# Weight gradients in pairs of accumulators over half tiles, more of them in each slot, and early places for the first loads of the attention backward

## The chip, the cores and the metric

The kernel runs on one core of a Trainium2 chip. The metric is the time of one execution on the device in microseconds (us): the median of three runs before the change is 865.62 us (864.01 to 870.82). A profile is one further execution, recorded by the hardware profiler; its span goes from the first to the last instruction. The engines are named as in the profile: PE is the matrix engine (PEld its weight loads), DVE the vector engine, ACT the scalar engine, POOL the general engine, SP the engine that only issues transfers (SPq is its queue). Transfers are issued by SP and by POOL, and move over 16 DMA engines that both share.

## The reference

A transformer layer with sliding-window attention and a feed-forward block is run forward, and all gradients of it are taken backward, on 2048 tokens of 512 features (bf16). Cut to what is computed:

```python
def A(x, wqkv, wo):                       # S=2048, D=512, 32 heads of 16
    q, k, v = split(x @ wqkv)
    idx = pos[:, None] - arange(8) * 2     # window of 8 keys, 2 apart
    attn = softmax(masked(einsum(q, k[idx]) * scale))
    return einsum(attn, v[idx]) @ wo

def B(x, w1, b1, w2, b2):                 # F = 1792
    return gelu(x @ w1 + b1) @ w2 + b2

def f(x, wqkv, wo, w1, b1, w2, b2):
    h = x + A(layernorm(x), wqkv, wo)
    return h + B(layernorm(h), w1, b1, w2, b2)

out, vjp = jax.vjp(f, x, wqkv, wo, w1, b1, w2, b2)
return (out, *vjp(grad_out))              # output and 7 gradients
```

## The kernel before

The tokens go in four chunks of 512 (`NC`, `CH`), each of four row tiles of 128. There are three stages.

The first stage runs the attention forward and leaves its intermediates in DRAM: the layer-normed inputs `ln1_d` and `ln2_d`, the attention output `o_d`, and the rows of q, k and v. The transposed `ln2` of each chunk stays in SBUF (`ln2T`, four tiles of the pool `lnT`).

The second stage is the feed-forward block, forward (`p2_h`) and backward (`p2_rest`). It stores the activations `g` and the gradient of their inputs `gh`, turned to token-major by a transposing DMA (`tok_store`, L508: SP reads into `tst`, POOL stores), in `gT_d` and `ghT_d`. At its end stand the gradient rows `gh_all`.

The third stage is the attention backward (from L612), and within it the weight gradients. In it the order on every engine is the order of the code (`tc.manual_schedule`), in the second stage a scheduler sets it. For each chunk `c`, DVE multiplies `got` (the gradient times `wo` transposed, made by `p3_go`) with the values `vw` (L888), PE sums the products into `ps_ga` (L894), DVE makes `pp`, PE takes off the row sum (L941), and DVE makes `glf` (L949), the gradient of the logits, and from it the coefficients `cf`. Then come band tiles: for v, q and k four each, in which DVE multiplies gathered rows `R` with `cf` (L793, two instructions a tile) and PE sums them (L801); `R` is 1.3 MB, gathered by an indirect DMA that POOL issues (L250). With a chunk's q, k and v done, `gln1` two passes later multiplies them with the transposed `wqkv` (L856) and runs the layer-norm backward on DVE. There are `NC + 2` passes, c = 0 to 5.

The weight gradients are plain matmuls over all 16 token tiles and nothing waits for them but the end. A generator, `wgrads` (L649), yields after each matmul; `filler` (L729) runs it until an allowance of time is spent, and `slot` (L752) grants that allowance: the time of the DVE work just issued, times `RATIO` (1.22), less the estimated time of the PE work that falls due in the slot. `MM` (0.22 us) is what a matmul of 512 columns is charged. In `wgrads`, `yield 24.0` or `yield 14.0` behind a load spends the allowance without a matmul, and `yield "q"` stops it until a flag of that name is set. What is left runs at the end (`filler(1000.0)`).

The order of the weight gradients is `out_6` (called gw2 below: L657, 14 groups of 16 matmuls), the bias `out_7` (16), `out_4` (gw1: L678, 28 groups of 16 with 256 columns), `out_3` (gwo: L691, 4 groups), `out_2` (gwq: L715, 12 groups). A group sums in one PSUM bank of two (`psF`), ACT copies it to one of two tiles `gwst` (L633), and POOL stores it (L634). One operand is a whole token-major tensor of 2 MB in a single buffer `r16` (`gout`, then `ln2`, `o`, `ln1`), the other comes in tiles of 1 MB in two buffers `gwm`. The `ln1` tensor is loaded in 32 transfers (L698), because its rows are permuted.

At the start of the third stage SP issues the transposed loads of `wo` and `wqkv` (L619, L621), then `vw` and `ln1r`.

Of the kernel before, what the change touches and what calls it, by code (L numbers as in the profile page):

```python
# [10 lines left out]
P = 128  # L11
BF16 = mybir.dt.bfloat16
# [24 lines left out]
def kernel(  # L37
# [277 lines left out]
    ln2T = [lnT.tile([P, DC, CH], BF16, name=f"ln2T{c}") for c in range(NC)]  # L315
# [181 lines left out]
    late.release()  # L497
    ff = LP("ff", "right")
# [6 lines left out]
    gh_all = [None] * NC  # L505
    ps2 = [dict() for _ in range(NC)]

    def tok_store(src, f0, f1, dst, c):  # L508
        n = f1 - f0
        st = ff.tile([P, 16, P], BF16, name="tst", tag="tst", bufs=3)  # L510
        SY.dma_start_transpose(out=st[:, 0:4 * n, :], in_=src[:, 0:n, :].rearrange("p a n -> p (a n)"))
        G.dma_start(out=dst[:, f0:f1, c, :], in_=st[:, 0:4 * n, :].rearrange("p (a t) f -> p a (t f)", a=n))  # L512

    def p2_h(c):
        d = ps2[c]
        d["g"], d["d"] = [], []
        for (f0, f1) in FB:
            n = f1 - f0
            xb = ff.tile([P, 4, 512], BF16, name="xb", tag="xb", bufs=2)
            x2 = ff.tile([P, 4, 512], BF16, name="x2", tag="x2", bufs=2)  # L520
# [28 lines left out]
    def p2_rest(c):  # L549
        d = ps2[c]  # L550
        gts, dts = d["g"], d["d"]
        goT = ff.tile([P, DC, CH], BF16, name="goT", tag="goT", bufs=1)
        SY.dma_start_transpose(out=goT[:], in_=gof[c * CH:(c + 1) * CH, :])
        gout = ff.tile([P, TPC, D], BF16, name="gout", tag="gout", bufs=1)
        load_rows(gout, gof, c)
        ln2 = ff.tile([P, TPC, D], BF16, name="ln2r", tag="ln2r", bufs=1)
# [55 lines left out]
    lnT.release()  # L612
# [5 lines left out]
    woT = p3.tile([P, DC, D], BF16, name="woT")  # L618
    SY.dma_start_transpose(out=woT[:], in_=A_wo)  # L619
    wqkvT = p3.tile([P, 12, D], BF16, name="wqkvT")  # L620
    SY.dma_start_transpose(out=wqkvT[:], in_=A_wqkv)  # L621
    glf = p3.tile([P, 2, SP], BF16, name="glf")
    V.memset(glf[:, :, S:SP], 0.0)
# [6 lines left out]

    def wg_out(ps, dst, width=D, sca=1.0):
# [15 lines left out]
    MM = 0.22  # L647

    def wgrads():  # L649
        r16 = load_tm("gout_r", gof)  # L650
        tiles = [load_t(gT_d, f) for f in range(2)]
        yield 24.0
        for f in range(FT):
            gtm = tiles[f // 2]
            ps = FY("ps_gw2")
            for t in range(NT):
                T.matmul(ps[:], lhsT=gtm[:, f % 2, t, :], rhs=r16[:, t, :], start=(t == 0), stop=(t == NT - 1))  # L657
                yield MM
            if f % 2 == 1:
                n = f // 2 + 2  # L660
                tiles.append(load_t(gT_d, n) if n < 7 else load_t(ghT_d, n - 7))
            wg_out(ps, out_6[f * P:(f + 1) * P, :], D, 0.5)
        ps = FY("ps_gb2")
        for t in range(NT):
            T.matmul(ps[0:1, :], lhsT=ones_col[:], rhs=r16[:, t, :], start=(t == 0), stop=(t == NT - 1))
            yield MM
        r16 = load_tm("ln2_r", ln2_d)
# [3 lines left out]
        yield 14.0  # L671
        tiles = tiles[7:]
        for q in range(7):
            ghm = tiles[q]
            for dc in range(DC):
                ps = FY("ps_gw1")
                for t in range(NT):
                    T.matmul(ps[:, 0:256].rearrange("p (a f) -> p a f", a=2), lhsT=r16[:, t, dc * P:(dc + 1) * P], rhs=ghm[:, :, t, :],  # L678
                             start=(t == 0), stop=(t == NT - 1))
                    yield MM / 2  # L680
                if dc == DC - 1:
                    if q + 2 < 7:
                        tiles.append(load_t(ghT_d, q + 2))
                    if q == 6:
                        r16 = load_tm("o_r", o_d)
                wg_out(ps, out_4[dc * P:(dc + 1) * P, q * 256:(q + 1) * 256], 256)
        yield 14.0
        for k in range(DC):
            ps = FY("ps_gwo")
            for t in range(NT):  # L690
                T.matmul(ps[:], lhsT=r16[:, t, k * P:(k + 1) * P], rhs=gh_all[t // TPC][:, t % TPC, :],  # L691
                         start=(t == 0), stop=(t == NT - 1))
                yield MM
            wg_out(ps, out_3[k * P:(k + 1) * P, :])
        r16 = gwp.tile([P, NT, D], BF16, name="ln1_r", tag="r16", bufs=1)
        for sc in range(NC * 2):
            for j, ap in enumerate(perm_rows(ln1_d, sc * 256, sc)):
                SY.dma_start(out=r16[32 * j:32 * j + 32, 2 * sc:2 * sc + 2, :], in_=ap)  # L698
        HN = NT // 2

        def half(sel, i):
            t_ = gwp.tile([P, HN, D], BF16, name="gqh", tag="gwm", bufs=2)
            SY.dma_start(out=t_[:], in_=g3_d[sel][:, i * HN:(i + 1) * HN, :])
            return t_
        yield "q"
        hv = [half(0, 0), half(0, 1)]
        yield 14.0
        for si, sel in enumerate((0, 2, 1)):
            for d2 in range(2):
                pss = [FY("ps_gwq") for _ in range(2)]  # L710
                for i in range(2):
                    for dd in range(2):
                        dc = 2 * d2 + dd
                        for t in range(HN):
                            T.matmul(pss[dd][:], lhsT=r16[:, i * HN + t, dc * P:(dc + 1) * P], rhs=hv[i][:, t, :],  # L715
                                     start=(i == 0 and t == 0), stop=(i == 1 and t == HN - 1))
                            yield MM
                        if i == 1:
                            wg_out(pss[dd], out_2[dc * P:(dc + 1) * P, sel * D:(sel + 1) * D])
            if si < 2:  # L720
                yield ("v", "k")[si]
                hv = [half((2, 1)[si], 0), half((2, 1)[si], 1)]
# [23 lines left out]
    RATIO = 1.22  # L746
# [28 lines left out]
    def load_R():  # L775
# [5 lines left out]
        R = p3.tile([P, 10, 512], BF16, name="R", tag="rows", bufs=3)  # L781
# [3 lines left out]
    def band_tile(kind, c, sc, m, cf, gs, sca, after):  # L785
# [4 lines left out]
        pr = p3.tile([P, 2, 4, 512], BF16, name="prb", tag="prod", bufs=3)  # L790
        for hf in range(2):
            o = (2 - 2 * hf if kind == "q" else 2 * hf) + 4 * m
            V.tensor_tensor(out=pr[:, hf].rearrange("p j (d h) -> p j d h", h=H),  # L793
# [3 lines left out]
        def pe():  # L797
            ps = Y("ps_band")
            for hf in range(2):
                for j in range(4):  # L800
                    T.matmul(ps[32 * j:32 * j + 32, :], lhsT=S32[:], rhs=pr[:, hf, j, :],  # L801
# [11 lines left out]
    st3 = [dict() for _ in range(NC + 2)]  # L813

    def p3_go(c, at=(1, 2, 3, 4)):
        ghT = p3.tile([P, DC, CH], BF16, name="ghT", tag="ghT", bufs=1)
        got = p3.tile([P, 4, CH], BF16, name="got", tag="got", bufs=1)
# [213 lines left out]
```

## Time and profile before

| what | value |
| --- | --- |
| median of the runs | 865.62 us (864.01 to 870.82) |
| the profiled execution's own time | 867.38 us |
| its span | 865.6 us |
| mean granted clock of PE | 0.896 of full speed |
| busy: PE, DVE, ACT, POOL | 661.8, 531.1, 339.7, 196.7 us |
| moved by DMA | 160.99 MB |
| second stage ends, third begins | about 432 us |
| last DVE work | about 719 us |

Rows of the timeline give the start and the length of a group of neighbouring instructions in us, the engine, the line of the code, the operation, output and inputs, how often, and in brackets how long the engine sat idle before it and what ended that. Rows of the waits give the engine and line that waited, what it waited for, and the total in us, the number of times and the longest. Rows of the windows give a stretch in us and its length, the busy time (and number of instructions) of PE, PEld, DVE, ACT and POOL, then the granted clock, the busy share of the 16 DMA engines, and GB/s. Line numbers are those of the kernel before.

### The profile page before, as it was taken

What the parts mean: (1) busy time and instruction counts of PE and PEld (TensorE: products, weight loads), DVE (VectorE), ACT (ScalarE), POOL (GpSimd) and SP (SyncE); (2) the same over time, 40 slices, a digit from 0 to 9 for tenths busy, and PEclk for the clock granted to TensorE, in tenths of its full rate; (3) what the DMA queues carried; (4) which work ended last, traced back from release to release, by engine and by line L of the source; (5) the groups of instructions that cost most, each with busy time, mean ns of one, the idle gap of its engine ahead of it and who ended that gap; (6) DMA issues with size and microseconds to landing.
All of it is one profiled execution on the core that took longest, in us unless ns stands there. A gap on an engine that the chain in (4) does not pass through costs nothing. (4 is left out here: it accounts for less than half of the span.)

```text
span 865.6 us, 10398 instructions
## 1 busy us (share of the span) xinstructions
PE 661.8 (76%) x3948; PEld 300.8 (35%) x3948; DVE 531.1 (61%) x774; ACT 339.7 (39%) x529; POOL 196.7 (23%) x253
## 2 busy tenths in 40 slices
PE   4888786667899898889935479888886798753486
PEld 2334332222333333333412134333322457631232
DVE  6889796478768777775615996977975951000000
ACT  2558675576446345342132144353323342100011
POOL 3204243301102102102100623243251323200011
PEclk9999998787999999999967569999986899977699
DMA  8547376785549558547996388678479544332442
GB/s 304 205 152 223 120 248 220 179 177 132 90 117 231 122 106 221 133 108 210 191 292 231 115 293 293 224 228 319 170 247 368 159 148 150 115 116 82 137 159 103
DMA packets 143120, 160.99 MB, mean 186 GB/s; under 512 B 95469, under 2 KB 125982, under 8 KB 136414
## 3 DMA queue, kind: packets, MB, share of 16 engines
q1 hardware_dynamic: 124846, 74.83, 33.3%
q0 software_dynamic: 18224, 85.49, 28.9%
q8 instruction: 31, 0.51, 0.2%
q14 instruction: 19, 0.16, 0.1%
HBM read 87.63 MB, written 48.03 MB: 157 GB/s over the span
## 5 line engine op out<-in xcount | busy, mean ns | idle before, releaser
L793 DVE TENSOR_TENSOR prb<-R,cf 128x2048 bf16<-128x2048 bf16 x96 | 110.5, 1218 | 16.9 <-DMA R<-q_d,rowi 13.9
L526 PE MATMUL ps_h<-ln2T,w 128*128 128x512 bf16 x224 | 65.2, 420 | 21.3 <-ACT x L529 18.7
L801 PE MATMUL ps_band<-prb,S 128*32 128x512 bf16 x384 | 41.1, 461 | 38.6 <-DVE prb L793 38.3
L715 PE MATMUL ps_gwq<-gqh,ln_r 128*128 128x512 bf16 x192 | 44.0, 390 | 30.4 <-DMA gqh<-gq_d 25.7
L634 POOL DMA_DIRECT2D out_dram<-gwst x58 | 31.5, 544 | 145.5 <-ACT gwst L633 136.0
L574 PE MATMUL ps_gg<-goT,w2T 128*128 128x512 bf16 x224 | 54.5, 378 | 11.0 <-DVE gb1p L577 8.6
L678 PE MATMUL ps_gw<-gwm,ln_r 128*128 128x256 bf16 x448 | 53.7, 279 | 7.8 <-ACT gwst L633 7.8
L657 PE MATMUL ps_gw<-gout_r,gwm 128*128 128x512 bf16 x224 | 58.3, 400 | 0.0
L561 PE MATMUL ps_f<-w,gt 128*128 128x512 bf16 x224 | 55.8, 393 | 1.6 <-DVE gt L538 1.6
L528 ACT ACTIVATE xb<-ps_h,b1c 128x512 bf16<-128x512 f32 x56 | 38.2, 686 | 45.9 <-PE ps_h L526 45.2
L351 PE MATMUL ps_qkv<-ln1T,wqkv 128*128 128x512 bf16 x192 | 48.6, 393 | 6.3 <-ACT kt L353 2.0
L211 ACT ACTIVATE gyr<-ps_gl,rstd 128x512 bf16<-128x512 f32 x32 | 22.0, 687 | 73.0 <-PE ps_gl L856 35.1
L678 PEld LDWEIGHTS <-ln_r 128*128 128x128 bf16 x448 | 43.9, 100 | 17.7 <-issue 11.8
L512 POOL DMA_DIRECT2D gT_d<-tst x16 | 12.6, 786 | 156.4 <-DMA tst<-gt 152.1
L888 DVE TENSOR_TENSOR pr<-got,vw 128x4096 bf16<-128x4096 bf16 x16 | 35.9, 2286 | 17.2 <-DMA vw<-vf_d 17.2
L856 PE MATMUL ps_gl<-wqkvT,gqkvT 128*128 128x512 bf16 x192 | 44.1, 385 | 0.0
L526 PEld LDWEIGHTS <-w 128*128 128x128 bf16 x224 | 23.3, 105 | 56.7 <-issue 39.5
L633 ACT ACTIVATE gwst<-ps_gw 128x256 bf16<-128x256 f32 (+1 forms) x42 | 18.9, 456 | 57.6 <-DMA out_dram<-gwst 30.1
L288 DVE TENSOR_TENSOR prb<-R,cf 128x2048 bf16<-128x2048 bf16 x32 | 37.3, 1210 | 5.7 <-DMA R<-v_d,rowi 2.9
L803 ACT ACTIVATE gks<-ps_band 128x512 bf16<-128x512 f32 x32 | 19.0, 600 | 53.9 <-PE ps_band L801 48.0
L258 DVE TENSOR_TENSOR pr<-qt,kt 128x4096 bf16<-128x4096 bf16 x16 | 36.0, 2282 | 5.5 <-ACT qt L353 3.4
L529 ACT ACTIVATE x<-ps_h,b1c 128x512 bf16<-128x512 f32 x56 | 38.1, 685 | 1.4 <-DVE dt__2685 L543 0.4
(327 smaller groups left out, 1207.2 us busy)
## 6 DMA issues: line engine op xcount, KB each, us to landing
gwm<-gT_d SPq DMA_DIRECT2D x7, 1024.0 KB
gwm<-ghT_d SPq DMA_DIRECT2D x7, 1024.0 KB
gT_d<-tst POOLq DMA_DIRECT2D x12, 512.0 KB
ghT_d<-tst POOLq DMA_DIRECT2D x12, 512.0 KB
ln_d<-ln POOLq DMA_DIRECT2D x8, 512.0 KB
out_dram<-gwst POOLq DMA_DIRECT2D x30, 128.0 KB
w<-in_B_w_dram POOLq DMA_DIRECT2D x2, 1792.0 KB
vw<-vf_d SPq DMA_DIRECT2D x4, 528.0 KB
```

The costliest lines, as they stand in the source:

```text
L351: T.matmul(ps[:, gg, :], lhsT=wqkv[:, dc, sel * D + g * P:sel * D + (g + 1) * P], rhs=st_[c]["ln1T"][:, dc, :], start=(dc == 0), stop=(dc ...
L526: T.matmul(ps[:, i, :], lhsT=w1[:, dc, f * P:(f + 1) * P], rhs=ln2T[c][:, dc, :], start=(dc == 0), stop=(dc == DC - 1))
L528: A.activation(out=xb[:, f - f0, :], in_=ps[:, i, :], func=ACT.Identity, bias=b1c[:, f:f + 1])
L529: A.activation(out=x2[:, f - f0, :], in_=ps[:, i, :], func=ACT.Square, bias=b1c[:, f:f + 1])
L561: T.matmul(ps[:], lhsT=gts[f // 4][:, f % 4, j * P:(j + 1) * P], rhs=w2[:, f, :], start=(f == 0), stop=False)
L574: T.matmul(ps[:, i, :], lhsT=w2T[:, dc, f * P:(f + 1) * P], rhs=goT[:, dc, :], start=(dc == 0), stop=(dc == DC - 1))
L657: T.matmul(ps[:], lhsT=gtm[:, f % 2, t, :], rhs=r16[:, t, :], start=(t == 0), stop=(t == NT - 1))
L678: T.matmul(ps[:, 0:256].rearrange("p (a f) -> p a f", a=2), lhsT=r16[:, t, dc * P:(dc + 1) * P], rhs=ghm[:, :, t, :], start=(t == 0), stop ...
L715: T.matmul(pss[dd][:], lhsT=r16[:, i * HN + t, dc * P:(dc + 1) * P], rhs=hv[i][:, t, :], start=(i == 0 and t == 0), stop=(i == 1 and t == ...
L793: V.tensor_tensor(out=pr[:, hf].rearrange("p j (d h) -> p j d h", h=H), in0=R[:, o:o + 4, :].rearrange("p j (d h) -> p j d h", h=H), in1=c ...
L801: T.matmul(ps[32 * j:32 * j + 32, :], lhsT=S32[:], rhs=pr[:, hf, j, :], start=(hf == 0), stop=(hf == 1), skip_group_check=True)
L856: T.matmul(ps[:], lhsT=gqkv[c][:, b, j * P:(j + 1) * P], rhs=wqkvT[:, b, :], start=(b == 0), stop=(b == 11))
```

## The change

**Pairs and halves.** The whole-tensor operand comes in two halves of eight token tiles (`load_half`, `load_perm`) in three buffers `r8`. `mm_pair` sums two groups at a time in the two PSUM banks: the first token half for both groups, then the second half for both. So the first half's buffer is free, and the next load can be issued, before the pair is done. Both groups are copied and stored when the pair is done.

**More matmuls per slot.** `RATIO` goes from 1.22 to 1.4, and of the yields that spend allowance only 10.0 before gwq and the two 6.0 stay; 24.0, 14.0 and 14.0 go.

**Early places.** The transposed `wo` and the three parts of the transposed `wqkv` take the places of the `ln2T` tiles in `lnT` once those are read, and are loaded during the second stage (`load_wT`). `glf` has a pool of its own. `vw`, the two halves of `gout` and the first two tiles of `gT_d` are the first loads of the third stage. `ln1r` is loaded a row tile at a time in three buffers instead of a chunk at a time in one. Temporaries of the second stage are merged (`xa`) and get fixed shapes.

```diff
+    def lnt(name):
+        return lnT.tile([P, DC, CH], BF16, name=name, tag="ln2T", bufs=NC)
...
+    def load_wT(name, src):
+        wT[name] = lnt(name)
+        SY.dma_start_transpose(out=wT[name][:], in_=src)
...
     for c in range(NC):
+        if c == 2:
+            load_wT("woT", A_wo)
+            load_wT("wqT", A_wqkv[:, 0:D])
+        if c == 3:
+            load_wT("wkT", A_wqkv[:, D:2 * D])
+            load_wT("wvT", A_wqkv[:, 2 * D:3 * D])
...
-    woT = p3.tile([P, DC, D], BF16, name="woT")
-    SY.dma_start_transpose(out=woT[:], in_=A_wo)
-    wqkvT = p3.tile([P, 12, D], BF16, name="wqkvT")
-    SY.dma_start_transpose(out=wqkvT[:], in_=A_wqkv)
...
-    def load_tm(name, src):
-        r = gwp.tile([P, NT, D], BF16, name=name, tag="r16", bufs=1)
-        SY.dma_start(out=r[:], in_=src.rearrange("(t p) d -> p t d", p=P))
+    def load_half(name, src, i):
+        r = gwp.tile([P, HN, D], BF16, name=name, tag="r8", bufs=3)
+        SY.dma_start(out=r[:], in_=src[i * HN * P:(i + 1) * HN * P, :].rearrange("(t p) d -> p t d", p=P))
...
+    def mm_pair(name, mm, cost):
+        pss = [FY(name) for _ in range(2)]
+        for i in range(2):
+            for o in range(2):
+                for t in range(HN):
+                    mm(pss[o], o, i, t, dict(start=(i == 0 and t == 0), stop=(i == 1 and t == HN - 1)))
+                    yield cost
+        return pss
...
+    load_vw(0)
+    gout_r = [load_half("gout_r", gof, 0)]
+    tiles = [load_t(gT_d, 0)]
+    gout_r.append(load_half("gout_r", gof, 1))
+    tiles.append(load_t(gT_d, 1))
 
     def wgrads():
-        r16 = load_tm("gout_r", gof)
-        tiles = [load_t(gT_d, f) for f in range(2)]
-        yield 24.0
...
+        ln2_r = [load_half("ln2_r", ln2_d, 0)]
+        for q in range(7):
+            g_ = tiles[q]
+            pss = yield from mm_pair("ps_gw2", lambda ps, o, i, t, k: T.matmul(ps[:], lhsT=g_[:, o, i * HN + t, :], rhs=gout_r[i][:, t, :], **k), MM)
+            n = q + 2
+            tiles.append(load_t(gT_d, n) if n < 7 else load_t(ghT_d, n - 7))
...
+        ln2_r.append(load_half("ln2_r", ln2_d, 1))
+        o_r = [load_half("o_r", o_d, 0)]
...
-        yield 14.0
...
+        o_r.append(load_half("o_r", o_d, 1))
+        ln1_r = [load_perm("ln1_r", ln1_d, 0)]
+        for k2 in range(2):
+            pss = yield from mm_pair("ps_gwo", lambda ps, o, i, t, k: T.matmul(
...
+        ln1_r.append(load_perm("ln1_r", ln1_d, 1))
         yield "q"
-        hv = [half(0, 0), half(0, 1)]
-        yield 14.0
+        hv = [load_g3(0, 0), load_g3(0, 1)]
+        yield 10.0
...
-    RATIO = 1.22
+    RATIO = 1.4
...
-    def load_ln1(c):
-        st3[c]["ln1"] = p3.tile([P, TPC, D], BF16, name="ln1r", tag="ln1r", bufs=1)
-        load_rows(st3[c]["ln1"], ln1_d, c)
+    def load_ln1(t):
+        x = pt3("ln1r")
+        SY.dma_start(out=x[:], in_=ln1_d[t * P:(t + 1) * P, :])
+        ln1q.append(x)
```

**What moves, place by place.** On SP, at the end of the second stage; `tst` are the last transposed stores, `go_d` the rows of the first chunk's `got`, `gwm` the 1 MB tiles. Before:

```order
75 L511 DMA_TRANSPOSE tst<-dt__3324 128x8x128
76 L619 DMA_TRANSPOSE woT<-in_A_wo_dram 128x4x512
77 L621 DMA_TRANSPOSE wqkvT<-in_A_wqkv_dram 128x12x512
78 L870 DMA vw<-vf_d 128x4x528
79 L178 DMA ln1r<-ln_d 128x4x512
80 L241 DMA go_d_144<-tmst 128x2x512 x2
81 L638 DMA gout_r<-in_grad_out_dram 128x16x512
```

And now:

```order
80 L531 DMA_TRANSPOSE tst<-dt__3317 128x8x128
81 L705 DMA vw<-vf_d 128x4x528
82 L671 DMA gout_r<-in_grad_out_dram 128x8x512
83 L683 DMA gwm<-gT_d 128x4096
84 L671 DMA gout_r<-in_grad_out_dram 128x8x512
85 L683 DMA gwm<-gT_d 128x4096
86 L892 DMA ln1r<-ln_d 128x512 x2
87 L241 DMA go_d_144<-tmst 128x2x512 x2
```

The two transposed loads no longer stand ahead of `vw`, and the first operands of the weight gradients stand ahead of the stores of `go_d`. On SP near the end; `ln_r` are the permuted halves of `ln1`, `gqh` the halves of gq, gv and gk for gwq, `sh` the shifted logits' gradient that the last k bands need. Before:

```order
112 L643 DMA gwm<-ghT_d 128x4096 x5
113 L638 DMA o_r<-o_d 128x16x512
114 L698 DMA ln_r<-ln_d 32x2x512 x32
115 L703 DMA gqh<-gq_d 128x4096 x2
116 L703 DMA gqh<-gv_d 128x4096 x2
117 L703 DMA gqh<-gk_d 128x4096 x2
```

And now:

```order
123 L884 DMA sh<-attn 32x2x512 x4
124 L671 DMA o_r<-o_d 128x8x512
125 L678 DMA ln_r<-ln_d 32x2x512 x16
126 L892 DMA ln1r<-ln_d 128x512 x4
127 L678 DMA ln_r<-ln_d 32x2x512 x16
128 L689 DMA gqh<-gq_d 128x4096 x2
129 L884 DMA sh<-glf 32x2x512 x4
```

The loads for gwo and gwq now stand among those of the passes c = 3 and c = 4, ahead of the last `sh`. On POOL, during the k bands of pass c = 2, where the rows for the v bands of chunk 2 are gathered ahead (`R<-go_d_146`, from the second gather before and the first now); `gk_d` and `gv_d` are stores of band results, `gx` those of the layer-norm backward, `gwst` those of the weight gradients. Before:

```order
113 L250 DMA R<-go_d_146,rowi 128x5120
114 L806 DMA gk_d<-gks 128x1024
115 L634 DMA out_dram<-gwst 128x512
116 L862 DMA out_dram<-gx 128x512
117 L634 DMA out_dram<-gwst 128x512
118 L862 DMA out_dram<-gx 128x512 x2
```

And now:

```order
113 L250 DMA R<-go_d_146,rowi 128x5120
114 L667 DMA out_dram<-gwst 128x256 x2
115 L850 DMA gk_d<-gks 128x1024
116 L667 DMA out_dram<-gwst 128x256 x2
117 L250 DMA R<-go_d_146,rowi 128x5120
118 L850 DMA gk_d<-gks 128x1024
```

The stores of gw1 (256 columns) now stand between the gathers, two at a time, where single stores of gw2 stood.

More of the change, by code (lines that the diff above doesn't have):

```diff
@@ L497 @@
     late.release()
+    glp = LP("glp", "right")
+    glf = glp.tile([P, 2, SP], BF16, name="glf")
+    V.memset(glf[:, :, S:SP], 0.0)
     ff = LP("ff", "right")
@@ L645, in load_t, with load_g3 @@
         return t_
-    MM = 0.22
-    def wgrads():
-        r16 = load_tm("gout_r", gof)
-        tiles = [load_t(gT_d, f) for f in range(2)]
-        yield 24.0
[L653 to L662, printed above, removed]
+    def load_g3(sel, i):
+        t_ = gwp.tile([P, HN, D], BF16, name="gqh", tag="gwm", bufs=2)
+        SY.dma_start(out=t_[:], in_=g3_d[sel][:, i * HN:(i + 1) * HN, :])
+        return t_
@@ L687, in wgrads @@
-        yield 14.0
[L688 to L704, printed above, removed]
+            g_ = tiles[7 + q]
+            for d2 in range(2):
+                pss = yield from mm_pair("ps_gw1", lambda ps, o, i, t, k: T.matmul(
+                    ps[:, 0:256].rearrange("p (a f) -> p a f", a=2), lhsT=ln2_r[i][:, t, (2 * d2 + o) * P:(2 * d2 + o + 1) * P],
+                    rhs=g_[:, :, i * HN + t, :], **k), MM / 2)
+                if d2 == 1 and q + 2 < 7:
+                    tiles.append(load_t(ghT_d, q + 2))
+                for o in range(2):
+                    dc = 2 * d2 + o
+                    wg_out(pss[o], out_4[dc * P:(dc + 1) * P, q * 256:(q + 1) * 256], 256)
@@ L705, in wgrads @@
+        ln1_r.append(load_perm("ln1_r", ln1_d, 1))
         yield "q"
[L706 to L707 removed]
+        hv = [load_g3(0, 0), load_g3(0, 1)]
+        yield 10.0
         for si, sel in enumerate((0, 2, 1)):
             for d2 in range(2):
[L710 to L719, printed above, removed]
+                pss = yield from mm_pair("ps_gwq", lambda ps, o, i, t, k: T.matmul(
+                    ps[:], lhsT=ln1_r[i][:, t, (2 * d2 + o) * P:(2 * d2 + o + 1) * P], rhs=hv[i][:, t, :], **k), MM)
+                for o in range(2):
+                    dc = 2 * d2 + o
+                    wg_out(pss[o], out_2[dc * P:(dc + 1) * P, sel * D:(sel + 1) * D])
```

123 lines of the change are left out of this document (70 added, 53 removed).

## The prediction

> **What bounds the kernel now.** I read the windows of the third stage first, then who waited for whom, then the timeline at the places of the longest waits.
>
> ```profile
> span 865.6 us, 10398 instructions
> ```
>
> ```profile
> 432.00:453.00 21.00, 7.04 (x35) 3.04 (x34) 2.67 (x9) 7.07 (x11) 2.02 (x2) 0.68 1.07 284
> ...
> 531.30:597.00 65.70, 56.08 (x386) 23.00 (x385) 54.79 (x57) 25.89 (x44) 24.11 (x24) 0.95 0.75 263
> 597.00:663.00 66.00, 52.97 (x340) 20.67 (x337) 49.56 (x53) 21.51 (x38) 21.80 (x25) 0.86 0.73 268
> ...
> 786.00:811.80 25.80, 0.09 (x2) 0.05 (x2) 0.00 (x0) 0.60 (x1) 0.54 (x1) 0.60 0.47 144
> ```
>
> The stage has three parts with different limits. From 432 to 453 PE and DVE are nearly idle and the DMA engines are full. In the passes (531 to 597 is c = 2) PE and DVE are both some 80% busy. After 722 DVE does nothing, and PE works off left-over weight gradients, with a stretch of 25.8 us in which it does nothing either.
>
> ```profile
> PE ps_gwq L715 <- DMA gqh<-gq_d: 25.7, 1, 25.7
> DVE pr L888 <- DMA vw<-vf_d: 17.2, 1, 17.2
> PE ps_gwo L691 <- DMA o_r<-o_d: 8.7, 1, 8.7
> PE ps_gw L678 <- ACT gwst L633: 7.8, 6, 4.2
> ```
>
> These four waits are loads and evictions that nothing covers. Since the weight gradients can go anywhere, the time is set by how much PE work is left when DVE is done, and by the waits.
>
> **The change part by part.** *The second stage* gets four transposed loads. One was:
>
> ```profile
> 425.01 3.17 SPq L619 DMA_TRANSPOSE woT<-in_A_wo_dram  x1
> 428.28 7.89 SPq L621 DMA_TRANSPOSE wqkvT<-in_A_wqkv_dram  x1
> 430.07 0.71 POOL L512 DMA_DIRECT2D ghT_d<-tst  x1 [1.18 <-issue]
> 436.06 0.59 ACT L830 CAST got<-ps_go 128x512 bf16<-128x512 f32 x1 [0.68 <-PE ps_go L828]
> 436.22 0.68 SPq L870 DMA_DIRECT2D vw<-vf_d  x1
> 452.76 8.90 DVE L888 TENSOR_TENSOR pr<-got,vw 128x4096 bf16<-128x4096 bf16 x4 [17.24 <-DMA vw<-vf_d]
> 471.00 1.03 PE L941 MATMUL ps_ga<-pp,nSum 128*128 128x512 bf16 x4
> 472.06 1.22 DVE L949 TENSOR_TENSOR glf<-ps_ga,attn 128x1024 bf16<-128x1024 f32 x1 [8.03 <-PE ps_ga L941]
> ```
>
> Four times 3.17 us of SP's queue would cost up to 12.7 if SP's `goT` loads came late for it; nothing is taken away there, so a gain is excluded. I take 0: the PE matmuls on `gt` between two chunks cover them, and the `tst` behind them feed only stores.
>
> *The start.* SP spends 7.89 us on `wqkvT`, then issues `vw` at 436.2, which lands 16.5 us later behind it. The last `tst` had landed by 430.07. Now `vw` follows the `tst` directly, so it should be there when the first `got` is, at 436.65. DVE starts 452.76 - 436.65 = 16.1 us sooner. On the way to the row sum, 21 matmuls of gw2 now stand on PE, 4.6 us at the rate below. The row sum of c = 0 starts at 471.00 - 16.1 + 4.6 = 459.5. These matmuls need the first halves: `vw` and two loads of 1 MB at 284 GB/s take 9 us, from 430 to 439, ahead of PE; the second halves come at about 447, just as PE wants them. If loads waited until 436, 4 us more: bounds 0 to 4, I take 0, since SP was free for `woT` at 425.0.
>
> *PE's work from there.* The rates, at full clock:
>
> ```profile
> 849.87 10.52 PE L715 MATMUL ps_gwq<-gqh,ln_r 128*128 128x512 bf16 x48 [0.56 <-DMA gqh<-gk_d]
> ```
>
> ```profile
> 731.81 7.15 PE L678 MATMUL ps_gw<-gwm,ln_r 128*128 128x256 bf16 x64 [0.51 <-ACT gwst L633]
> ```
>
> ```profile
> 701.59 0.62 PE L801 MATMUL ps_band<-prb,S 128*32 128x512 bf16 x8
> 702.14 2.47 PE L678 MATMUL ps_gw<-gwm,ln_r 128*128 128x256 bf16 x21
> 704.45 0.61 PE L305 MATMUL ptu<-ident,gks 128*128 128x128 bf16 x8
> 704.89 0.38 PE L678 MATMUL ps_gw<-gwm,ln_r 128*128 128x256 bf16 x2
> ```
>
> That is 0.219 us for 512 columns, 0.112 for 256, 0.55 for a group of 8 band matmuls, 0.44 for 8 transposes. Behind the first row sum stand, in the new order, 715 matmuls of 512 columns (156.6 us), 448 of gw1 (50.2), 60 groups of 8 (33.0) and 32 of transposes (14.1): 253.9 us. With the larger ratio these fill the slots: pass c = 2, counted in this way, gets 58.7 us of PE work where it had 50.2, against 54.8 us of DVE, so PE is now the longer engine in the passes.
>
> *What PE must still wait for.* Once a pass the row sum and what follows go from PE to DVE and back:
>
> ```profile
> 476.52 0.40 PE L801 MATMUL ps_band<-prb,S 128*32 128x512 bf16 x4 [4.49 <-DVE prb L793]
> ...
> 558.88 1.02 PE L941 MATMUL ps_ga<-pp,nSum 128*128 128x512 bf16 x4 [0.94 <-DVE pp L936]
> ...
> 565.47 0.40 PE L801 MATMUL ps_band<-prb,S 128*32 128x512 bf16 x4 [2.66 <-DVE prb L793]
> ...
> 567.15 2.59 PE L657 MATMUL ps_gw<-gout_r,gwm 128*128 128x512 bf16 x6
> ```
>
> No filler is put between these, so the wait stays: 4.5 for c = 0, and per pass 0.9 + 0.7 + 2.7 = 4.3 (0.7 inside the band tile), three times: 17.4 us. DVE also waits for gathers:
>
> ```profile
> DVE prb L793 <- DMA R<-q_d,rowi: 13.9, 4, 5.8
> ```
>
> The same gathers now run beside loads that stood in the tail. With PE the longer engine, DVE's lead, up to the three buffers of products, covers these waits, so I take 0; without that cover they cost PE the 13.9 us again. Behind the wait at 565.47 six matmuls took 2.59 us where six at 0.219 are 1.3: the clock has to come back, about 1.1 us beside the last one's drain, four times 4.5. [...]
>
> *The end of the passes.* In c = 4 the gate q is passed, but `yield 10.0` and the loads leave PE without filler in the v bands.
>
> ```profile
> 786.08 20.30 SPq L698 DMA_DIRECT2D ln_r<-ln_d  x32
> 806.49 1.01 SPq L703 DMA_DIRECT2D gqh<-gq_d  x2
> ```
>
> ```profile
> 811.76 15.68 PE L715 MATMUL ps_gwq<-gqh,ln_r 128*128 128x512 bf16 x64 [25.71 <-DMA gqh<-gq_d]
> ```
>
> The second half of `ln1` waits for PE's 48th gwo matmul, then takes 16 x 0.634 = 10.1 us of SP, and gq lands 5.3 us after its issue: 15.4 us. SP's last `sh` queues behind, and DVE's k bands wait for it. Meanwhile PE has 16 gwo matmuls (3.5 us) and four v tiles, at DVE's pace of
>
> ```profile
> 475.28 9.13 DVE L793 TENSOR_TENSOR prb<-R,cf 128x2048 bf16<-128x2048 bf16 x8
> ```
>
> 2.3 us a tile, after two layer-norm tiles and `cf` on DVE. I count 8 us idle in the v tiles and 3 until gq and the first k tile: 11 us, between 0 (the loads land within the v tiles and DVE is ahead) and 25.7 (nothing covered). Nearer to the middle, since half of the load now stands ahead.
>
> *The tail.* gv and gk still load into two buffers:
>
> ```profile
> PE ps_gwq L715 <- DMA gqh<-gv_d: 2.5, 2, 1.6
> PE ps_gwq L715 <- DMA gqh<-gk_d: 2.2, 2, 1.6
> ```
>
> 4.7 us stays. PE's last matmul ends at 860.4, the span at 865.6: 5.2 us.
>
> *Stores.* Both accumulators and both `gwst` are now in use at once, so a pair can't be evicted until the stores of the pair before have landed, and ACT stands on that wait with band evictions queued behind it.
>
> ```profile
> 524.86 0.60 ACT L633 ACTIVATE gwst<-ps_gw 128x512 bf16<-128x512 f32 x1 [0.31 <-PE ps_gw L657]
> ...
> 538.37 0.60 ACT L633 ACTIVATE gwst<-ps_gw 128x512 bf16<-128x512 f32 x1 [5.63 <-DMA out_dram<-gwst]
> ```
>
> ```profile
> 528.19 1.78 POOL L250 DMA_INDIRECT R<-go_d,rowi  x1 [3.92 <-DVE prb L793]
> ```
>
> ```profile
> 731.38 0.66 ACT L633 ACTIVATE gwst<-ps_gw 128x256 bf16<-128x256 f32 x2 [3.09 <-PE ps_gw L678]
> 733.97 0.38 ACT L633 ACTIVATE gwst<-ps_gw 128x256 bf16<-128x256 f32 x1 [1.94 <-DMA out_dram<-gwst]
> ```
>
> A slot was free again 1.9 us after its eviction in the tail, but 13.5 us after the start of one behind a gather. The 14 pairs of gw1 now run among the gathers, one per 6.1 us of PE work (85.4 us in their stretch). So each costs 0 to 7.4 us, together 0 to 104. The passes had:
>
> ```profile
> ACT gwst L633 <- DMA out_dram<-gwst: 9.5, 3, 5.6
> ```
>
> (from 495 to 720), for 24 evictions; 28 of gw1 at that rate give 11 us, which I take, because that row is from the same mix of gathers and stores.
>
> Sum: 459.5 + 253.9 + 17.4 + 4.5 + 11 + 4.7 + 5.2 + 11 = 767 us of span. The profiled execution took 867.38 with a span of 865.6, and the median of the runs is 865.62, so I read the span as the median: **767 us**.
>
> **The rivals.**
>
> *Packed.* The stores land in time and gq within the v tiles: 767 - 11 - 8 = 748. For it: PE has slack between pairs whenever bands stand there. Against: the row of 538.37. 0.18.
>
> *Moved, not hidden.* The passes were already as long as DVE, PE and the gathers together make them (65.7 us with each only 55 busy), and grow by all the filler they get. Then only waits go: 11.5 at the start, 8.7, 25.7 - 11, and 7.8: 865.6 - 42.7 = 823. For it: the 10 us of each pass that neither engine fills. Against: PE idles in them only at the row sum and where DVE is late. 0.12.
>
> *Stores behind gathers.* Half of the 104 us comes: 756 + 52 = 808, 790 to 840. POOL issues gathers and stores in one queue, and DVE is busy throughout. 0.14. [...]
>
> *Slower.* Every round trip is the 13.5 us seen: 104 for gw1, and 7 x 2.5 = 18 for gw2 (its pairs 11 us apart): 756 + 122 = 878. It turns slower from a mean wait of 110 / 21 = 5.2 us a pair. Only one such wait is in the trace. 0.04.
>
> **How the numbers follow.** The forecast has 0.52, about 755 to 790. 740 to 822 takes in the packed case, most of the stores' case and part of the moved case, and leaves out about 2 in 10. A measurement tells about 1% from no change (857 to 874): faster takes all but the slower rival and a little between, 0.95; same 0.02; slower 0.03.
>
> **What would show it.** Right: `pr` starts near 437 with no wait for `vw`; no wait of `ps_gwo` for `o_r`; gwo done before DVE ends; a wait of PE before gwq of under 12 us; the last 130 or so gwq matmuls alone after DVE. The forecast is wrong by the stores if ACT waits for `out_dram<-gwst` more than 30 us in all, by the passes if c = 2 is longer than 74 us, and at the start if `vw` or `gout_r` is waited for.

## The result and the profile after

The median went from 865.01 us (864.01 to 870.82, four runs) to **809.11 us** (807.85 to 810.59, four runs): a ratio of 0.934, with a 95% interval of 0.930 to 0.939. The profiled execution of the changed kernel took 809.62 us with a span of 807.8. The forecast was 767 with a range of 740 to 822: sign and range hold, the likeliest value is 42 us too low. Of the runs below, three of the kernel before and two of e7 (809.9 and 811.3 us) were in a slower state and are left out of the ratios.

The page of the changed kernel, its line of the span:

```profile
span 807.8 us, 10432 instructions
```

Its windows, with the columns of the windows above: first the third stage as a whole from 436 us to the end, then the passes c = 2 and c = 4, and the tail.

```profile
436.00:807.80 371.80, 300.51 (x2038) 146.68 (x2035) 213.29 (x225) 118.55 (x215) 89.51 (x124) 0.91 0.65 224
...
544.81:623.87 79.06, 65.78 (x524) 37.66 (x522) 52.50 (x54) 27.70 (x53) 21.38 (x31) 0.91 0.75 251
...
697.43:754.96 57.53, 40.89 (x233) 17.14 (x231) 30.08 (x38) 16.95 (x31) 10.86 (x14) 0.76 0.46 160
754.96:807.80 52.84, 41.56 (x190) 18.15 (x188) 8.06 (x22) 10.82 (x24) 8.10 (x15) 0.97 0.36 118
```

The same window of the kernel before:

```profile
436.00:865.60 429.60, 310.19 (x2030) 151.04 (x2027) 209.58 (x218) 117.55 (x210) 105.22 (x122) 0.84 0.58 197
```

What PE waited for in that window, the six longest of the changed kernel and, behind them, the two of the kernel before that the prediction did not show:

```profile
PE ps_band L845 <- DVE prb L837: 25.3, 16, 6.3
PE ps_gw L736 <- ACT gwst L666: 13.3, 9, 7.6
PE ps_gwq L759 <- DMA gqh<-gq_d: 4.4, 1, 4.4
PE ps_gwq L759 <- DMA gqh<-gk_d: 4.1, 2, 2.6
PE ps_go L871 <- ACT ghT L190: 3.4, 4, 2.0
PE ps_gw L718 <- ACT gwst L666: 2.5, 4, 1.0
```

```profile
PE ps_band L801 <- DVE prb L793: 38.3, 32, 5.8
...
PE ps_ga L894 <- DVE pr L888: 22.9, 9, 13.2
```

All rows of PE in this view, the small ones too, add up to 113.7 us before and 66.0 us after. With PE's busy time and the 5.2 us behind its last matmul they give the stage: 300.5 + 66.0 + 5.2 = 371.7 of 371.8 us after, and 310.2 + 113.7 + 5.2 = 429.1 of 429.6 before. So the window got 57.8 us shorter: 47.7 of waits and 9.7 of busy time for the same matmuls, at a granted clock of 0.91 in place of 0.84. I use this account below. Busy time, waits and end are all the time there is, so that it closes proves no cause; that is left to the experiments.

In c = 2 and c = 4 the longest waits were these; first PE, then POOL and ACT around 604, then DVE, SP and PE in c = 4:

```profile
576.58 0.62 PE L845 MATMUL ps_band<-prb,S 128*32 128x512 bf16 x4 [2.25 <-DVE prb L837]
577.72 0.62 PE L845 MATMUL ps_band<-prb,S 128*32 128x512 bf16 x4 [0.52 <-DVE prb L837]
578.27 3.59 PE L736 MATMUL ps_gw<-gwm,ln_r 128*128 128x256 bf16 x16
...
598.08 1.92 PE L736 MATMUL ps_gw<-gwm,ln_r 128*128 128x256 bf16 x16
...
613.46 2.93 PE L736 MATMUL ps_gw<-gwm,ln_r 128*128 128x256 bf16 x13 [7.63 <-ACT gwst L666]
```

```profile
602.95 2.00 POOL L250 DMA_INDIRECT R<-go_d,rowi  x1 [2.48 <-DVE prb L837]
604.95 1.10 POOL L667 DMA_DIRECT2D out_dram<-gwst  x2
```

```profile
613.02 0.66 ACT L666 ACTIVATE gwst<-ps_gw 128x256 bf16<-128x256 f32 x2 [7.96 <-DMA out_dram<-gwst]
```

```profile
735.02 1.97 DVE L272 STREAM_TRANSPOSE cf<-sh 128x1024 bf16<-128x1024 bf16 x1 [12.87 <-DMA sh<-glf]
```

```profile
708.42 10.28 SPq L678 DMA_DIRECT2D ln_r<-ln_d  x16
718.86 1.28 SPq L689 DMA_DIRECT2D gqh<-gq_d  x2
722.76 2.53 SPq L884 DMA_DIRECT2D sh<-glf  x4
```

```profile
727.18 4.00 PE L759 MATMUL ps_gwq<-gqh,ln_r 128*128 128x512 bf16 x9 [4.36 <-DMA gqh<-gq_d]
...
738.36 0.62 PE L845 MATMUL ps_band<-prb,S 128*32 128x512 bf16 x4 [6.33 <-DVE prb L837]
```

Two stores of gw1 issued behind a gather at 604.95 let go of their `gwst` tiles only 8 us later, and PE stood for 7.6. The last `sh` stands on SP behind half of `ln1` and both halves of gq, as the prediction had it; DVE waited 12.9 us for it and PE 6.3. Behind some waits the matmuls are slow for a while: 16 of gw1 took 3.59 us at 578.27 and 1.92 at 598.08. The granted clock fell within the wait of 2.25 us (0.59 in the window 576.0 to 576.5) and was 0.50 from 576.5 to 582.8; through a wait of 2.55 us before 508.76 it stayed at 1.00.

### The profile page after: what moved, and what is told of

The parts are those of the page before. It is cut to its first block, busy times and chain, and to the rows that moved or that the text cites. A ratio compares the mean times of both kernels' runs of the same rounds, so it can differ in the third digit from the quotient of the medians.

```text
span 807.8 us, 10432 instructions
## 1 busy us (share of the span) xinstructions
PE 649.9 (80%) x3948; PEld 296.0 (37%) x3948; DVE 532.3 (66%) x774; ACT 337.6 (42%) x529; POOL 179.5 (22%) x253
## 5 line engine op out<-in xcount | busy, mean ns | idle before, releaser
L736 PE MATMUL ps_gw<-gwm,ln_r 128*128 128x256 bf16 x448 | 59.7, 287 | 13.8 <-ACT gwst L666 13.3
L549 ACT ACTIVATE xb<-ps_h,b1c 128x512 bf16<-128x512 f32 x56 | 38.3, 687 | 44.9 <-PE ps_h L547 44.8
L759 PE MATMUL ps_gwq<-gqh,ln_r 128*128 128x512 bf16 x192 | 47.3, 401 | 10.2 <-DMA gqh<-gq_d 4.4
L211 ACT ACTIVATE gyr<-ps_gl,rstd 128x512 bf16<-128x512 f32 x32 | 21.9, 686 | 80.2 <-PE ps_gl L902 42.1
L845 PE MATMUL ps_band<-prb,S 128*32 128x512 bf16 x384 | 34.3, 418 | 25.4 <-DVE prb L837 25.3
L306 ACT COPY gqkvT<-ptu 128x1024 bf16<-128x1024 bf16 x24 | 24.3, 1012 | 51.5 <-PE ptu L305 51.4
L547 PEld LDWEIGHTS <-w 128*128 128x128 bf16 x224 | 23.0, 103 | 59.6 <-issue 41.6
L219 DVE CUSTOM_DVE_ANT_0 junk<-gyr,ln1r 128x512 bf16<-128x512 bf16 x16 | 11.1, 691 | 47.6 <-ACT gyr L211 47.5
L556 ACT ACTIVATE xa<-xa 128x2048 bf16<-128x2048 bf16 (+1 forms) x16 | 27.2, 1698 | 29.9 <-DVE xa L555 29.9
```

Of the source, the lines that this page charges most:

```text
L547: T.matmul(ps[:, i, :], lhsT=w1[:, dc, f * P:(f + 1) * P], rhs=ln2T[c][:, dc, :], start=(dc == 0), stop=(dc == DC - 1))
L549: A.activation(out=xb[:, f - f0, :], in_=ps[:, i, :], func=ACT.Identity, bias=b1c[:, f:f + 1])
L736: pss = yield from mm_pair("ps_gw1", lambda ps, o, i, t, k: T.matmul(ps[:, 0:256].rearrange("p (a f) -> p a f", a=2), lhsT=ln2_r[i][:, t, ...
L759: pss = yield from mm_pair("ps_gwq", lambda ps, o, i, t, k: T.matmul(ps[:], lhsT=ln1_r[i][:, t, (2 * d2 + o) * P:(2 * d2 + o + 1) * P], rh ...
```

## The experiments

Theory: from the first row sum on PE is the longer engine (DVE is busy for 52.5 of the 79.1 us of c = 2), and time is PE's work, its waits and the slow clock behind them. The rivals stand with each run. All times are medians; the line numbers in the rows are those of each kernel.

| run | us | ratio to the kernel before, 95% | PE busy from 436 us | PE waits |
| --- | --- | --- | --- | --- |
| the changed kernel | 809.1 | 0.930 to 0.939 | 300.5 | 66.0 |
| e1, ratio 1.22 | 822.3 | 0.944 to 0.955 | 304.2 | 76.9 |
| e2, more store tiles | 799.1 | 0.918 to 0.929 | 300.0 | 55.5 |
| e3, last shift early | 799.5 | 0.918 to 0.930 | 298.4 | 57.2 |
| e6, filler behind row sums | 793.5 | 0.909 to 0.922 | 292.6 | 56.8 |
| e8, e2 + e3 + e6 | 777.1 | 0.893 to 0.907 | 290.0 | 41.5 |
| e10, no pairs | 820.0 | 0.942 to 0.958 | 305.4 | 72.0 |
| e11, no early homes | 827.7 | 0.947 to 0.964 | 303.1 | 83.8 |
| e12, e8 with ratio 1.22 | 791.7 | 0.907 to 0.923 | 293.0 | 58.0 |

**e1: the ratio alone goes back.**

```diff
-    RATIO = 1.4
+    RATIO = 1.22
```

> Only the ratio goes back from 1.4 to 1.22. A slot of 2.45 us then gets 0.44 us less of weight gradients, about 8 us a pass in c = 1 to 3, 25 us in all, which must run in c = 4 or after DVE's end. Theory (in the changed kernel PE is the longer engine: DVE is busy for 52.5 of 79.1 us of c = 2, so each pass lasts as long as PE's work and its waits): the passes get shorter by what they lose, and the time changes by the waits alone: PE's waits for products grow by about 10 us as before the change, the waits of c = 4 (6.3, 4.4 and 2.0 us) shrink: 805 to 820. Rival (the larger slots hide work under DVE): all 25 us come on top after DVE's end: 830 to 838.

Measured 822.3 us: 13 us more, between the two. Rows of its windows (c = 2, and from the end of c = 4) and of PE's waits:

```profile
543.02:613.45 70.43, 57.50 (x398) 25.55 (x396) 53.73 (x55) 26.97 (x47) 17.67 (x25) 0.90 0.84 285
...
730.69:823.00 92.31, 68.34 (x299) 29.45 (x297) 8.06 (x22) 14.72 (x30) 11.34 (x21) 0.91 0.39 130
```

```profile
PE ps_band L845 <- DVE prb L837: 15.5, 12, 4.5
PE ps_gw L736 <- ACT gwst L666: 14.8, 8, 5.1
PE ps_gwq L759 <- DMA gqh<-gq_d: 12.4, 1, 12.4
PE ps_gw L718 <- ACT gwst L666: 9.7, 4, 7.8
```

The passes c = 1 to 4 take 243.7 us (487 to 730.69) in place of 267.5 (487.5 to 754.96), 23.8 less, and PE is busy in them for 22.0 us less (198.7 for 220.7): they shrink by about what they lose, as the theory has it. The tail grows by 39.5, of which 26.8 are this work moved (68.3 us busy for 41.6) and 12.6 are waits, above all for gq (12.4, where nothing is left to do). In the passes PE's waits for DVE's products did not grow, in the whole stage they fell from 25.3 to 15.5; what grew were those for `gwst`, from 18.9 to 31.7 over all rows. That step of my expectation was wrong.

**e2: the stores get room.** Three tiles `gwst`, and a pair of gw1 shares one.

```diff
-    gwp.tile([P, D], BF16, name="gwst", tag="gwst", bufs=2)
+    gwp.tile([P, D], BF16, name="gwst", tag="gwst", bufs=3)
...
+    st = gwp.tile([P, D], BF16, name="gwst", tag="gwst", bufs=3)
     for o in range(2):
         dc = 2 * d2 + o
-        wg_out(pss[o], out_4[...], 256)
+        A.activation(out=st[:, o * 256:o * 256 + 256], in_=pss[o][:, 0:256], func=ACT.Copy, scale=1.0)
+        G.dma_start(out=out_4[...], in_=st[:, o * 256:o * 256 + 256])
```

> Three tiles gwst in place of two, and the two groups of a gw1 pair share one tile, so that three pairs and not one can be on their way to DRAM. Theory (stores that land late hold the accumulators, and PE is the longer engine): ACT's wait for out_dram<-gwst goes from 17.4 us to under 3, PE's waits for gwst go from 18.8 us (13.3, 2.5, 2.0 and the slow clock behind the longest) to under 5, and the time goes to 790 to 797. Rival (the transfers are late because the DMA engines are full, and PE has other waits directly behind): ACT's wait goes, but the time stays at 803 to 810.

Measured 799.1 us. ACT's wait for the stores is down to 0.3 us, and c = 2 from 79.1 to 68.6, but the time gained is 10 us and not the 12 to 19 expected. Late stores cost about 10 us, no more.

**e3: the last shift ahead of the loads.**

```diff
+            if c == NC - 1:
+                sh_last.append(shift(c, glf))
...
-            shk = shift(c - 1, glf)
+            shk = sh_last[0] if c == NC else shift(c - 1, glf)
```

> The last shift of the logits' gradient (sh<-glf of chunk 3) is issued at the end of pass 3, ahead of the second half of ln1 and the loads of gq on SP's queue. Theory (SP's order makes the late wait): DVE's wait of 12.9 us for sh goes, and with it PE's 6.3 us wait for the first k tile and most of the slow clock behind it; the 4.4 us wait for gq stays or grows by 1: 800 to 804, with the last DVE work 8 to 13 us earlier. Rival (PE's tail sets the end, and what is not done in c = 4 waits for the loads of gv and gk all the same): DVE's wait goes, PE's waits for gqh grow by as much: 807 to 810.

Measured 799.5 us, just under the theory's 800. DVE's wait for `sh` is gone, c = 4 goes from 57.5 to 48.7 us, and PE's wait for gq grows only from 4.4 to 5.5. The order on SP cost about 10 us.

**e4 and e7: the transposed loads leave the second stage.** In e4 the four calls of `load_wT` stand behind the second stage's code:

> The four transposed loads stand at the start of the third stage again, ahead of vw. Theory (the loads on SP's queue and the DMA engines made the second stage longer): its last gyr is back from 436.9 to about 432.6 us; the loads then delay the start of the third stage by up to 12 us (SP's 3.2 and 7.9 us and vw behind them): 808 to 817. Rival (the merged tiles xa and xb, which stay here, made it longer): the last gyr stays at about 437 and the third stage starts later still: 816 to 822.

809.1 us, and no load went to the third stage: the trace of e4 has those of `wq`, `wk` and `wv` at 271.1, 336.9 and 407.3 us, the changed kernel at 271.5, 335.9 and 399.9: the scheduler of the second stage issued them at the same places, although the calls stood elsewhere. So it tells nothing, though 809.1 lies within the expectation. e7 puts three of them behind the `gwm` loads, in the part whose order is that of the code:

> Three of the four transposed loads (wq, wk, wv; 4.2, 4.8 and 3.9 us of SP's queue) now really stand in the third stage, behind the first loads of the weight gradients; the load of wo stays in the second stage, and nothing else changes. Theory (they hold up SP's queue in the second stage): the last gyr comes at 432 to 434 us in place of 436.9, the third stage starts as much sooner, and as wq is wanted only in c = 2, the time is 804 to 807. Rival (the merged tiles or the clock made the second stage longer): the last gyr stays within 1 us of 436.9 and the time at 808 to 812.

The last `gyr` of the second stage, in the changed kernel, e7 and e11 (below):

```profile
436.92 0.69 ACT L211 ACTIVATE gyr<-ps_gl,rstd 128x512 bf16<-128x512 f32 x1 [2.01 <-PE ps_gl L606]
```

```profile
433.20 0.69 ACT L211 ACTIVATE gyr<-ps_gl,rstd 128x512 bf16<-128x512 f32 x1 [2.01 <-PE ps_gl L606]
```

```profile
433.39 0.69 ACT L211 ACTIVATE gyr<-ps_gl,rstd 128x512 bf16<-128x512 f32 x1 [2.01 <-PE ps_gl L606]
```

In the ten kernels that have the changed second stage with all four loads it comes at 436.9 to 440.2, in the two without three (e7) or all (e11) of them at 433.2 and 433.4: the theory holds, and the loads cost about 4 us there. That size is rough, since the kernel before and e9, with one and the same second stage, end it 6.8 us apart. The queue shows how. The load of `goT` for the last chunk on SP, in the changed kernel and in e11:

```profile
385.68 2.06 SPq L573 DMA_TRANSPOSE goT<-in_grad_out_dram  x1
```

```profile
380.50 1.76 SPq L573 DMA_TRANSPOSE goT<-in_grad_out_dram  x1
```

The `goT` load ahead of the one of wq starts together in both (256.0 and 256.2), the one behind it 2.5 us later than in e11, and this one, behind wk too, 5.2 us later. e7's time does not decide between the two expectations: its runs of 796.4, 799.2 and 803.8 us have the median 799.2, below both, and two others took 809.9 and 811.3. In the profiled one (811.3) the first row sum came 5.1 us sooner (461.07 for 466.17), and the third stage lost this again, PE standing for `gwst` (24.0 us in all for 18.9) and for gq (6.4 for 4.4).

**e5: ACT issues the stores.**

```diff
-        G.dma_start(out=dst, in_=st[:, 0:width])
+        A.dma_start(out=dst, in_=st[:, 0:width])
```

> The stores of gwst are issued by ACT itself, behind its eviction, in place of POOL; there are still two tiles gwst. Theory (a store stands in POOL's queue behind gathers, or behind other work of POOL): ACT's wait for out_dram<-gwst falls from 17.4 us to under 5 and the longest from 8.0 to under 3; time 793 to 800, as with more tiles. Rival (the DMA engines are full with the 1 MB load of the next operand tile and a gather, whoever issues the store): the wait stays at 12 to 20 us, and the time at 804 to 812.

```profile
ACT gwst L666 <- DMA out_dram<-gwst: 18.7, 7, 4.2
```

807.1 us and 18.7 us of waiting: as the main cause, POOL's queue falls. The longest wait is shorter (4.2 for 8.0), and so may be the sum: it was 17.4 in the changed kernel, but 27.9 in e4, in which POOL issues the same stores, so single profiles don't settle it. The time is what the rival had. In the changed kernel the 16 DMA engines were 84% busy while the stores issued at 604.95 were on their way (window of that stretch, columns as above), so the transfer itself may be late whoever issues it:

```profile
604.95:613.02 8.07, 0.88 (x9) 0.64 (x7) 3.60 (x3) 0.11 (x1) 1.62 (x4) 0.83 0.84 288
```

**e6: filler for the time of `glf` and `cf`.**

```diff
             cfq = coefs(p3, glf[:, 0, 0:1], c * CH, SP)
+            filler(3.2)
```

> 3.2 us more of weight gradients right behind each pass's row sum, for DVE's glf and cf (1.2 and 2.0 us), which no slot pays for; none is left out elsewhere. Theory (PE idles there although other work for it stands by, and then runs slow): PE's wait for the first product behind the row sum (4.5 us in c = 0, 2.3 to 2.6 in c = 1 to 3) goes to under 1 us in each pass and the slow matmuls behind it (3.6 us for 16 of gw1 in place of 1.9) with it: 10 to 16 us less, 793 to 800. Rival (what PE gains there it loses in c = 4, which then finds less filler, and at the stores): 803 to 810.

793.5 us, as the theory had it. The first wait behind the row sum is at most 0.35 us in c = 1 to 3, and 2.35 are left of 4.48 in c = 0. PE's waits for products go from 25.3 to 16.6, though one wait for `gwst` of 10.5 us appears, and the busy time falls by 8 us with the clock (0.94 from 436 us in place of 0.91).

**e8: e2, e3 and e6 together.**

> Three gwst tiles with a shared one for each gw1 pair, the early last shift, and the 3.2 us of filler behind each row sum together. Theory (PE is the longer engine from the first row sum on, so waits taken away from it add up): 809 less 10, 10 and 10 to 16 is 773 to 780. Rival (the gq loads set when the end can begin, whatever is saved before them): PE's wait for gqh<-gq_d grows by 5 to 15 us and the time is 785 to 795.

```profile
436.00:773.80 337.80, 289.98 (x2014) 145.62 (x2041) 214.30 (x228) 118.74 (x216) 95.12 (x125) 0.95 0.71 248
```

```profile
PE ps_band L847 <- DVE prb L839: 13.2, 14, 3.1
PE ps_gw L736 <- ACT gwst L744: 4.8, 6, 1.4
PE ps_gwq L761 <- DMA gqh<-gq_d: 4.4, 1, 4.4
```

777.1 us (775.6 to 781.3), 0.900 of the kernel before and 777.1 / 809.1 = 0.960 of the changed one. The gains nearly add up (10 + 9.6 + 15.6 = 35 for 32), and gq's wait has not grown: the theory, and not the rival. PE's waits fell by 24.5 us, the profiled span by 34.0: a microsecond of waiting costs 34.0 / 24.5 = 1.4, the rest being clock (0.91 to 0.95).

**e9: the ratio alone, in the kernel before.** The same line, from 1.22 to 1.4.

> The kernel before with the ratio 1.4 in place of 1.22 and nothing else of the change. Theory (the work per slot is one part of the gain, worth the 13 us that it is worth in the changed kernel, but here the single 2 MB buffer still makes PE wait for o, ln1 and gq, and these waits only come sooner): 850 to 862. Rival (the larger slots are worth nothing without the half tiles, since whatever PE gains it spends on the next 2 MB load): 863 to 870.

```profile
PE ps_gwq L715 <- DMA gqh<-gq_d: 25.8, 1, 25.8
PE ps_band L801 <- DVE prb L793: 21.9, 20, 4.5
...
PE ps_gwo L691 <- DMA o_r<-o_d: 7.7, 1, 7.7
```

843.6 us, a ratio of 0.979 (0.969 to 0.989): better than both expectations. The loads are waited for as before (25.8 and 7.7 us); PE's waits for products fall from 38.3 to 21.9. So in the kernel before the larger slots did cover time in which PE stood for DVE. Not all of the gain is theirs: in this profile the second stage, which the ratio does not touch, ended 6.8 us sooner (last `gyr` at 425.76 for 432.56) and the first row sum came 11.2 us sooner; from there on it took 378.7 us for 394.6, 15.9 less, with 9.2 us less of PE waits, as those for `gwst` grew from 7.8 to 13.0.

**e10: no pairs.** One group after the other, with the half tiles kept.

```diff
-        for i in range(2):
-            for o in range(2):
+        for o in range(2):
+            for i in range(2):
```

> The changed kernel with the matmuls of a pair of accumulators one group after the other (16 for the first, then 16 for the second) in place of 8 and 8 by token halves; half tiles, loads and ratio stay. Theory (a pair ends with both accumulators taken, so PE stands until ACT has emptied one; single groups end apart, and the first is emptied beside the second's matmuls): PE's waits for gwst go from 18.8 us to under 12, those for half tiles grow by a few: 802 to 809. Rival (the pairs carry part of the gain, since a single group wants both halves at once): waits for gout_r, ln_r, o_r and gqh grow by over 5 us: 812 to 822.

820.0 us, 11 more (14 by the ratios, as the kernel before ran at 861.8 us beside it): the rival. PE's waits for `gwst` stay (11.8 for 13.3 in gw1), those for gq, gv and gk go from 9.2 (4.4, 0.7 and 4.1) to 18.3 (7.9, 5.5 and 4.9).

**e11: no early homes.** The two transposed loads stand in `p3` ahead of `vw` again, `lnT` is released as before.

```diff
-    woT = wT["woT"]
-    wqkvT = [wT[n] for n in ("wqT", "wkT", "wvT")]
+    woT = p3.tile([P, DC, D], BF16, name="woT")
+    SY.dma_start_transpose(out=woT[:], in_=A_wo)
+    wq3 = p3.tile([P, 12, D], BF16, name="wqkvT")
+    SY.dma_start_transpose(out=wq3[:], in_=A_wqkv)
+    wqkvT = [wq3[:, 4 * i_:4 * i_ + 4, :] for i_ in range(3)]
```

> The four transposed loads stand where they stood before the change, at the start of the third stage in buffers of its own, ahead of vw; all else is the changed kernel. Theory (the loads cost the second stage 4 us, and their early places save the wait for vw): the last gyr comes at about 433 in place of 436.9, DVE's first pr waits 12 to 17 us for vw, the first row sum comes 5 to 9 us later than 466.2, and the time is 812 to 819. Rival (PE is the longer engine anyway and fills the wait with weight gradients): 806 to 811.

```profile
429.07 19.33 SPq L641 DMA_TRANSPOSE wqkvT<-in_A_wqkv_dram  x1
```

```profile
461.34 8.90 DVE L927 TENSOR_TENSOR pr<-got,vw 128x4096 bf16<-128x4096 bf16 x4 [25.00 <-DMA vw<-vf_d]
```

827.7 us, 18.6 more, beyond the theory's 819: the direction is shown, the size was missed, with the row sum 17.7 us later (483.87) and not 5 to 9: the transposed load held SP for 19.3 us where it held it for 7.9 in the kernel before and for 9.0 in e9. Why is open. So the 18.6 us are more than what the early places save against the kernel before.

**e12: e8 with the ratio 1.22.**

> The three edits together (777 us) with the ratio 1.22. Theory (PE is the longer engine and the ratio only decides where the weight gradients stand; with the waits for stores and row sums gone less is lost either way, but gq's load then waits for gwo to end): 777 to 786. Rival (the larger slots hide work under DVE whatever the waits): 13 us more as in the changed kernel, or the whole 25: 788 to 802.

791.7 us, 14.6 more than e8 and within the rival's numbers, in part by its mechanism. SP's load of the second half of `ln2` in e8, then in e12, and e12's waits:

```profile
546.35 0.37 SPq L671 DMA_DIRECT2D ln_r<-ln_d  x1
```

```profile
563.21 3.06 SPq L887 DMA_DIRECT2D sh<-glf  x4
566.37 1.27 SPq L671 DMA_DIRECT2D ln_r<-ln_d  x1
```

```profile
PE ps_gw L736 <- DMA ln_r<-ln_d: 11.5, 1, 11.5
PE ps_band L847 <- DVE prb L839: 11.4, 13, 2.8
PE pgb L1035 <- DVE gb1b L1033: 8.0, 1, 8.0
```

PE's waits for products are no longer than in e8 (11.4 for 13.2). With smaller slots the generator reaches the load 20 us later, behind a shift on SP, and PE meets it: 11.5 us. And PE stands 8.0 us for DVE's last result (`gb1b`) with all 192 matmuls of gwq behind it; in e8 larger slots had put 116 of them ahead, PE came there at 748.9, 5 us after DVE, and did not wait. Those 8.0 us are the rival's, work that the slots would have hidden. So the ratio does two things here: it decides where on the queues the loads come to stand, and how much filler is left to cover DVE's end. In e1 `gb1b` is not waited for; there it is gq's wait and the stores' that grew.

## Why the prediction was right and wrong

The sum from the first row sum on was 767 - 459.5 = 307.5 us. Measured were 807.8 - 466.17 = 341.6: 278.1 of PE busy, 58.3 of its waits and 5.2 at the end.

- **The second stage, taken as 0** (bounds 0 to 12.7): about 4 us (436.92 for 433.20 in e7 and 433.39 in e11). The cover I named, PE's matmuls on `gt`, did not hold: SP's `goT` loads did come late, by 2.5 and 5.2 us, and the stage never makes it up.
- **The start:** `vw` is not waited for, as said, nor `gout_r`. `pr` starts 452.76 - 441.46 = 11.3 us sooner, not 16.1 and not near 437; the difference is mainly the second stage. A load that I had not named, `gwm` (2.3 us), and slow matmuls behind it (9 in 4.02 us, at a granted clock of 0.50) bring the row sum to 466.17, 6.7 us behind 459.5:

```profile
441.46 8.90 DVE L929 TENSOR_TENSOR pr<-got,vw 128x4096 bf16<-128x4096 bf16 x4 [1.60 <-ACT got L873]
```

```profile
451.09 4.02 PE L718 MATMUL ps_gw<-gout_r,gwm 128*128 128x512 bf16 x9 [2.27 <-DMA gwm<-gT_d]
...
466.17 1.03 PE L982 MATMUL ps_ga<-pp,nSum 128*128 128x512 bf16 x4
```

- **PE's work and the clock:** this term failed most. 253.9 us at full clock and 4.5 for four ramps make 258.4; PE was busy 278.1 at a granted clock of 0.92, 19.7 more. I had counted four ramps, one a pass; slow matmuls stand behind other waits too (at 613.46 and 727.18, both at a granted clock of 0.50). The 16 at 578.27 alone lost 3.59 - 1.92 = 1.7 us, not my 1.1; there the clock fell within a wait of 2.25 us, and it had stayed at 1.00 through one of 2.55.
- **Stores, 11 us:** PE's four rows of waits for `gwst` are 13.3, 2.5, 1.8 and 1.0, 18.6 in all; ACT's wait for the stores was 17.4, under the 30 that I had set as the mark of the rival, though e4 came near it with 27.9. e2 gives 10 us for taking them away.
- **Row sums 17.4 and the end of the passes 11:** together 28.4; measured 25.3 for products and 4.4 for gq, 29.7. The sum held in part by luck: without c = 4 the waits for products were 14.6, less than the 17.4, and in c = 4 they were 10.8, with gq 15.2 in place of 11. The last `sh` behind SP's loads was as told, and could have been avoided (e3), as could most of the row sums (e6).
- **Tail loads 4.7 and the end 5.2:** 4.8 and 5.2. **Waits that I had not counted** (`gqkvT`, `gb1b`, `o_r` and others): 5.1.

So 767 + 6.7 (start) + 19.7 (clock) + 7.6 (stores) + 1.3 + 0.1 + 5.1 = 807.5.

Of the marks set: gwo was done at 711.8, before DVE; PE waited 4.4 us for gq, under 12; some 127 gwq matmuls ran alone at the end. `o_r` was still waited for, 1.2 us. c = 2 took 79 us and so passed the 74 that were to show the forecast wrong by the passes; in e2, without the stores' waits, it took 68.6. Yet it is not the moved-not-hidden rival (823): that has PE idle for DVE in the grown passes, and PE's waits for products fell from 38.3 to 25.3. The stores' rival gave 808, the measured number, by a mechanism that cost 10 us and not 52; its number is right by chance. Its queue on POOL falls with e5 as the main cause: with ACT issuing, the wait was 18.7 us for 17.4, and the time 807.1 for 809.1.

Undone one at a time, the parts are worth 13 us (ratio, e1), 11 (pairs, e10) and 19 (early homes, e11), 43 of the 56; the rest was not separated. These are no clean shares: of the 19, some 11 may be the load that held SP for 19.3 us in place of 7.9, and the 13 hang on where the loads and stores came to stand. What is open: how much the merged tiles of the second stage cost or save, since its end varied from 425.8 (e9) to 432.6 with the code of the kernel before.

## What to carry to other kernels

When work is moved under a longer engine, count that engine's time as its busy time at the granted clock, its waits and its end: a microsecond of waiting more or less moved the stage by 1.1 us (e2) to 1.8 (e6 and e10), in e8 by 1.4. Filler belongs exactly where the engine waits (behind a row sum, e6), and the amount of filler also decides where its loads stand on SP's queue, which was worth 11.5 us in e12. A call moved in the code is not yet an instruction moved: read its start from the trace.

## What the runs showed of the hardware

- Stores issued by ACT were waited for 18.7 us (e5), the same stores issued by POOL 17.4 (the changed kernel) and 27.9 (e4). In the changed kernel two stores of 64 KB, issued at 604.95, took 8 us, with the DMA engines 84% busy.
- The same transposed load of 1.5 MB held SP's queue for 7.9 us in the kernel before, 9.0 in e9 and 19.3 in e11.
- In the changed kernel the granted clock fell to 0.50 in a wait of 2.25 us before 576.58, stayed there until 582.8, and left 16 matmuls near half rate (3.59 us for 1.92). In a wait of 2.55 us before 508.76 it stayed at 1.00.
